# Three small changes around the edges of a tuned kernel: other buffers for the first weights, one product moved up, the last store cut in two

## The chip, the cores and the metric

The kernel runs on one core of one Trainium2 chip. The metric is the device time of that core in microseconds (us), taken over several executions. Every time below was taken beside executions of the kernel before, on the same chip.

In the trace of before, TensorE has 6856 matmul records and as many weight loads, VectorE 998 instructions (696 of them TENSOR_TENSOR), ScalarE 667 (all but one ACTIVATE or COPY) and GpSimd 318 (304 TENSOR_TENSOR). Of the 612 instructions that queue transfers, 562 are SyncE's, 42 ScalarE's and 8 GpSimd's. In the profile PE is TensorE, DVE is VectorE, ACT is ScalarE, POOL is GpSimd, SP is SyncE, and a "q" behind a name means that engine's sequencer.

## The reference

```python
kv  = np.einsum('bhsd,bhse->bhde', k, v)        # batch 8, heads 8, seq 576, head dim 64
out = np.einsum('bhsd,bhde->bhse', q, kv)
rms = np.sqrt(np.mean(out * out, axis=-1, keepdims=True) + 1e-06)
x   = (out / rms * g_norm)                      # -> 4608 x 512
h   = x @ w_in                                  # 512 x 2048, float64 in memory
g   = np.maximum(0.01 * h, h)
y   = g @ w_out                                 # 2048 x 512, float64 in memory
```

## The kernel before

The two weight matrices lie in memory as float64. They are brought in as 32 raw tiles of 512 KB ("load 0" to "load 31"), and each is turned into float32 by a "rounding": ScalarE makes two tensors from the raw words (`add` and `cut`), then VectorE needs four steps for the result. Loads with odd numbers (and 0, but not 31) are tiles of `w_in`, brought by four transfers each; the others are tiles of `w_out`, brought by one. There are seven raw buffers ("homes"), so load j can be issued only after rounding j−7 has read its words:

```python
raw_homes = itertools.cycle([view(stage, i * NW, NW) for i in range(3)]
                            + [pair(i, NW) for i in range(4)])
...
def round_f64(dst, raw):
    ...
    pin(nc.scalar.activation(add, lo, func=AF.Copy, scale=2.0 ** -29))
    pin(nc.scalar.activation(cut, hi.bitcast(F32), func=AF.Copy, scale=2.0 ** -112))
    ...                     # four pinned VectorE steps
```

The four `pair` buffers first hold k and v of the last two pairs of heads of the first batch. Loads 1 and 2 were queued before that batch's kv products (the first part of its attention), loads 3 to 6 after them:

```python
for j in range(1, 3):
    load_w(j)
...                                   # transposes of q
for m in range(2):
    ...
    attention_kv(0, m, kv_ps)
for j in range(3, 7):
    load_w(j)
...
square(1, 1)
spread(0)
add_up(1, 1)
root(1)
```

The first block of tokens then runs in 17 steps. Step n multiplies x by one tile of `w_in` (`h_ps`), applies the leaky relu (a "Prelu" on ScalarE, written `g_n` below), and adds step n−1's product with `w_out` (`o_acc`); the attention of the next batch (batch 1) is spread over the steps. Between the products, `between` issues loads, records roundings, and spreads the attention of the next batch (batch 1) over the steps.

```python
act = nc.scalar.activation(gT, h_ps, func=AF.Prelu, alpha=SLOPE)
if n == 2 * NC * U - 1:
    pin(act)                          # only the last Prelu is pinned
...
while half and rounded < min(3 * n + 8, 2 * n + 13, len(w_jobs) - (n < 11)):
    if loaded < len(w_jobs):
        load_w(loaded)
        loaded += 1
        if loaded in (15, 19):
            load_pair(1, (loaded - 15) // 4)     # q, k, v of batch 1
    round_w(rounded)
    rounded += 1
```

`pin` keeps an instruction in program order among the pinned ones.

Of the kernel before, what the change touches and what calls it, by code (L numbers as in the profile page):

```python
# [23 lines left out]
def kernel(  # L24
# [36 lines left out]
    nc = tc.nc  # L61
    B, H, S, D = q.shape
    DM, DF = w_in.shape
    P = 128
# [6 lines left out]
    NB = B * S // NT  # L71
    N2 = NT // 2
    U = 2
    NC = DF // 2 // (U * P)
# [24 lines left out]
    NW = U * NE * P  # L99
    w1_all = consts.tile([P, 2 * NC * NW], F32, name="w1_all")  # L100
    stage = consts.tile([P, 3 * NW], F32, name="stage")
# [3 lines left out]
    def view(t, lo, *shape):  # L105
        n = 1
        for d in shape:
            n *= d
        t = t[:, lo:lo + n]
        names = "abcd"[:len(shape)]  # L110
        return t.rearrange(f"p ({' '.join(names)}) -> p {' '.join(names)}",
                           **dict(zip(names, shape))) if len(shape) > 1 else t

    def pair(i, *shape):
        return view(pairs, i * NW, *shape)

    def matmul(*args, **kw):
        pin(nc.tensor.matmul(*args, **kw))  # L118
# [86 lines left out]
    def spare(n, name, dtype=F32):  # L205

        return gpool.tile([P, n], dtype, tag=next(spare_homes), name=name)

    raw_homes = itertools.cycle([view(stage, i * NW, NW) for i in range(3)]
                                + [pair(i, NW) for i in range(4)])  # L210

    def load(t, src, eng):

        if len(src.shape) == len(t.shape):
            t, src = [t], [src]
        else:
            n = src.shape[1]
            t = [t[i * n:(i + 1) * n] for i in range(src.shape[0])]
        for i, (to, part) in enumerate(zip(t, src)):
            pin(eng[i * len(eng) // len(t)].dma_start(to, part))  # L220

    def load_f64(src, eng):
        a, n = src.shape[-2:]
        n //= 2
        raw = next(raw_homes).bitcast(U32).rearrange("p (n two) -> p n two", two=2)
        load(raw.rearrange("p (a n) two -> p a (n two)", a=a), src, eng)
        return raw
# [41 lines left out]
    def load_w(j, *eng):  # L269
        eng = eng or (nc.sync,)  # L270
        dst, src = w_jobs[j]
        if w_in.dtype == I64:
            w_raws[j] = load_f64(src.bitcast(U32), eng)
        else:
            load(dst, src, eng)
# [33 lines left out]
    def attention_kv(b, m, kv_ps):  # L309

        two = [(k_ins.pop((b, p)), v_ins.pop((b, p)), p) for p in (2 * m, 2 * m + 1)]
        for j in range(J):
            for i in range(2):
                for k_in, v_in, p in two:
                    r, c = 64 * i, 64 * half_of(p, i)
                    matmul(kv_ps[p % 2][c:c + 64, m, :], lhsT=k_in[r:r + 64, j, :],
                           rhs=v_in[r:r + 64, j, :], start=(j == 0), stop=(j == J - 1))
# [125 lines left out]
    def first_attention():  # L443
# [11 lines left out]


        rest = ps_m.tile([64, NP, P], F32, tag="oc", name="rest_ps")
        for j in range(1, 3):
            load_w(j)

        def move(p, l, to, of):

# [5 lines left out]
        for p in range(NP):  # L468
# [3 lines left out]
            for j in range(J):  # L472
                to = banks[j // 4][:, j % 4, :] if j < 8 else rest[:, p, :]
# [9 lines left out]
        for m in range(2):  # L483
            if m:
                keep_warm()
            attention_kv(0, m, kv_ps)
        for j in range(3, 7):
            load_w(j)
        w0 = rounding(0)
        next(w0, None)  # L490
# [19 lines left out]
        def square(half, l):  # L510
            pin(nc.scalar.activation(squares[half][l], o_ps[half][l], func=AF.Square))
# [9 lines left out]
        def add_up(half, l):  # L521

            for e in range(2):
                matmul(sum_ps[half][E * l:E * l + E, :N2], lhsT=group,
                       rhs=squares[half][l][:, e, :], start=(e == 0), stop=(e == 1))

        def root(half):

            pin(nc.scalar.activation(flat[half], sum_ps[half][:64, :N2], func=AF.Sqrt,
                                     scale=1.0 / D, bias=eps_sb[:64]))  # L530
# [13 lines left out]
        def spread(half):  # L544

            for l in range(2):
                for t in range(2):
                    for p in range(NP):
                        matmul(inv_ps[half][E * p:E * p + E, l, t * P:t * P + P],
                               lhsT=roots[half][:, t, l, p:p + 1].to_broadcast([P, E]),  # L550
                               rhs=ident, start=True, stop=True)
# [17 lines left out]
        for _ in w0:  # L569
            pass  # L570
        square(1, 1)
        spread(0)
        add_up(1, 1)
        root(1)
        turn(1)
        keep(1, 0)
# [11 lines left out]
    def add(eng, out_, a, b_, minus=False, pinned=False):  # L588
        ins = eng.tensor_tensor(out_, a, b_, op=ALU.subtract if minus else ALU.add)  # L589
        if pinned or steady and eng is nc.vector:  # L590
            pin(ins)
# [49 lines left out]
    ORDER = (1, 2, 6, 5, 7, 3, 4)  # L641
# [201 lines left out]
    def product_o(n, g_sides, os, finish):  # L843
        c = n % NC
        w_sides, _ = sides_w2(n)
        sums = sides_w2(n + 1)[1] if n + 1 < NC * (NB - 1) else lambda i: None
        if c == 0:
            for key in ("11", "12", "21", "22"):
                os[key] = opool.tile([P, 2, N2], F32, tag="o", name=f"o{key}", bufs=6)

        into = {1: ("11", True), 5: ("22", True), 2: ("11", False), 6: ("12", True),
                3: ("12", False), 7: ("22", False), 4: ("21", True)}

        def done(i, bank):
            key, fresh = into[i]
            to = os[key].rearrange("p u (v n) -> p (u v) n", v=2)
            if c == 0 and fresh:
                nc.scalar.copy(to, bank)
            else:
                add(nc.vector, to, bank, to)  # L860
            if c == NC - 1 and i in (2, 7, 3, 4):
                finish(key, os[key])

            if i == 5:
                sums(0)
            elif i == 4:
                sums(1)


        yield from strassen((("oa", "oc"), ("oc", "oa"))[n % 2], lambda i, part, r: g_sides[i][:, 2 * r + part, :],  # L870
                            lambda i, part, r: w_sides[i][:, r, :], done)
# [5 lines left out]
            n = None if n is None else n - 1  # L877

    def store(i):
        def finish(key, o):  # L880
            r0 = i * NT + (int(key[0]) - 1) * N2
            c0 = (int(key[1]) - 1) * N2
            nc.scalar.dma_start(
                out[r0:r0 + N2, c0:c0 + N2].rearrange("(t p) m -> p t m", p=P), o)
        return finish

    def first_block(between):
# [28 lines left out]
        for t in range(4):  # L916
# [5 lines left out]
            nc.scalar.dma_start(out[t * P:(t + 1) * P, :], o)  # L922

    first_attention()
    steps = {i: tail for tail in [tail_of(0, NT, S)] for i in (6, 8, 10)}
    a_steps = attention(1, False)
# [50 lines left out]
    for i in range(1, NB):  # L977
# [3 lines left out]
        os = {}  # L981
# [96 lines left out]
```

## Time and profile before

| | before |
|---|---|
| median of three runs | 932.22 us (930.87 to 932.27) |
| span of the profiled run | 929.0 us, mean granted clock 0.999 |
| first feed-forward product (`h_ps`) starts | 26.78 us |
| second kv product of batch 1 (its last two pairs of heads) | 91.55 us, its v landed at 88.92 us |
| last matmul ends | 924.12 us |

A line of the timeline reads: start, duration, engine, source line, operation, output and inputs, shapes, how many, and in brackets how long the engine had stood idle before it and what released it. The prediction shows the lines of the opening. The list of TensorE's waits has the waited-for operation, us in total, number of times, longest.

One line of the list of TensorE's waits: waited-for operation, us in total, number of times, longest.

```profile
PE h_ps L118 <- DVE w_all L255: 0.2, 1, 0.2
```

Before the change a rounded weight is waited for once, for 0.2 us.

### The profile page before, as it was taken

The page shows a single profiled execution, that of the slowest core. Times are in us where ns is not written, and L with a number is a line of the kernel's source. Part 1 is how long each engine was busy: PE and PEld are TensorE (multiplying, and loading weights), DVE is VectorE, ACT ScalarE, POOL GpSimd, SP SyncE. Part 2 cuts the span into 40 slices and gives each one's busy share as a digit, 9 for nine tenths or more (in the row PEclk, how much of TensorE's full clock was granted, in tenths as well). Part 3 has the DMA queues.
Part 4 walks back from the last instruction along what each step waited for, and adds up shares of the span by engine and source line. Part 5 has one row for each costly group of instructions (what it writes and reads, how often), then busy time and mean ns, then how long its engine had stood idle before and what let it go on. Part 6 is the DMA issues. An engine that isn't in the chain of part 4 may idle for free.

```text
span 929.0 us, 17587 instructions
## 1 busy us (share of the span) xinstructions
PE 918.4 (99%) x6856; PEld 776.2 (84%) x6856; DVE 619.2 (67%) x998; ACT 331.0 (36%) x667; POOL 319.0 (34%) x318
## 2 busy tenths in 40 slices
PE   8999999999999999999999999999999999999997
PEld 5544447888998999899989999899988999999996
DVE  4866995586456876597756874687568744654554
ACT  4544632242134332532343423342343333223330
POOL 2000364977522532226211711272225322532222
PEclk9999999999999999999999999999999999999999
DMA  9999926895597679856995599658655676667632
GB/s 258 226 246 239 217 99 199 275 298 165 193 323 245 184 206 300 267 175 190 284 289 180 172 281 293 202 179 256 229 168 177 197 219 185 186 199 221 189 111 91
DMA packets 90066, 200.03 MB, mean 215 GB/s; under 512 B 9856, under 2 KB 42112, under 8 KB 89984
## 3 DMA queue, kind: packets, MB, share of 16 engines
q1 hardware_dynamic: 79392, 186.85, 68.5%
q10 hardware_dynamic: 10144, 10.88, 3.4%
q8 instruction: 55, 0.90, 0.4%
q0 software_dynamic: 448, 1.18, 0.3%
q14 instruction: 27, 0.22, 0.1%
HBM read 172.39 MB, written 26.48 MB: 214 GB/s over the span
## 4 chain that ended last, share of the span: by engine, by line
PE 95%; DMA 2%; DVE 2%; issue 0%; ACT 0%; POOL 0%; ACTq 0%; DVEq 0%; POOLq 0%
PE o_a L118 21%; PE o_c L118 21%; PE h_ha L118 11%; PE h_hb L118 8%; PE h_hc L118 8%; PE h_hd L118 6%; PE o_acc L118 6%; PE h_ps L118 6%; PE o_ps L118 2%; PE kv_ps L118 2%; PE h_a L118 1%; PE h_b L118 1%; DMA pairs<-in_v_dram 1%; PE h_c L118 1%; PE h_d L118 1%; DMA pairs<-in_moe_w_out_dram 1%
## 5 line engine op out<-in xcount | busy, mean ns | idle before, releaser
L589 POOL TENSOR_TENSOR gs<-g 128x512 f32<-128x512 f32 x64 | 81.3, 1289 | 442.9 <-ACT g L760 442.9
L589 DVE TENSOR_TENSOR o<-o_c,o 128x512 f32<-128x512 f32 x104 | 71.6, 689 | 111.8 <-PE o_c L118 111.8
L760 ACT ACTIVATE g<-g 128x512 f32<-128x512 f32 x124 | 78.2, 631 | 120.5 <-DVE g L589 120.5
L824 ACT COPY w_all<-h_ha 128x512 f32<-128x512 f32 x84 | 48.7, 580 | 187.9 <-PE h_ha L118 179.2
L589 DVE TENSOR_TENSOR o<-o_a,o 128x512 f32<-128x512 f32 x88 | 60.5, 687 | 68.0 <-PE o_a L118 67.9
L118 PE MATMUL o_c<-pairs,gs 128*128 128x256 f32 x384 | 91.3, 381 | 0.0
L118 PE MATMUL o_a<-pairs,gs 128*128 128x256 f32 x384 | 90.8, 379 | 0.0
L118 PEld LDWEIGHTS o_c<-pairs,gs 128*128 128x128 f32 x384 | 69.8, 190 | 9.3 <-issue 1.4
L118 PEld LDWEIGHTS o_a<-pairs,gs 128*128 128x128 f32 x384 | 69.8, 190 | 7.8
L118 PE MATMUL o_c<-w,g 128*128 128x256 f32 x256 | 61.6, 383 | 0.0
L118 PE MATMUL o_a<-w,g 128*128 128x256 f32 x256 | 61.6, 383 | 0.0
L118 PEld LDWEIGHTS h_ha<-stage,w_all 128*128 128x128 f32 x448 | 58.7, 192 | 2.8
L118 PE MATMUL h_ha<-stage,w_all 128*128 128x128 f32 x448 | 59.0, 275 | 0.0
L118 PE MATMUL h_ps<-xT,w_all 128*128 128x512 f32 (+1 forms) x136 | 57.9, 570 | 0.2 <-DVE w_all L255 0.2
L118 PE MATMUL o_acc<-w,g 128*128 128x512 f32 x128 | 58.0, 597 | 0.0
L589 DVE TENSOR_TENSOR g<-g,pairs 128x512 f32<-128x512 f32 x84 | 55.6, 689 | 1.9
L118 PEld LDWEIGHTS o_a<-w,g 128*128 128x128 f32 x256 | 46.4, 190 | 11.4 <-ACT pairs L824 2.7
L589 POOL TENSOR_TENSOR pairs<-w_all 128x512 f32<-128x512 f32 x8 | 11.1, 1386 | 123.3 <-DMA stage<-in_moe_w_in_dram 95.4
L118 PEld LDWEIGHTS o_c<-w,g 128*128 128x128 f32 x256 | 46.4, 190 | 5.8
L118 PEld LDWEIGHTS h_ps<-xT,w_all 128*128 128x128 f32 x136 | 25.5, 190 | 29.2 <-issue 26.5
L589 DVE TENSOR_TENSOR g<-w_all 128x512 f32<-128x512 f32 x28 | 21.8, 780 | 40.9 <-ACT w_all L824 40.9
L589 DVE TENSOR_TENSOR w_all<-h_hc,w_all 128x512 f32<-128x512 f32 x56 | 38.4, 686 | 15.3 <-PE h_hc L118 15.0
(193 smaller groups left out, 2039.3 us busy)
## 6 DMA issues: line engine op xcount, KB each, us to landing
w_all<-w SPq DMA_DIRECT2D x196, 448.0 KB, 4.1
pairs<-w SPq DMA_DIRECT2D x56, 512.0 KB, 4.4
out_dram<-o ACTq DMA_DIRECT2D x36, 256.0 KB, 4.6
v_in<-in_v_dram SPq DMA_DIRECT2D x29, 288.0 KB, 5.6
k_in<-in_k_dram SPq DMA_DIRECT2D x28, 288.0 KB, 5.8
q_in<-in_q_dram SPq DMA_DIRECT2D x56, 144.0 KB, 6.4
q_in<-in_q_dram SPq DMA_DIRECT2D x56, 140.0 KB, 6.3
w<-stage SPq DMA_DIRECT2D x12, 512.0 KB, 4.6
```

The source lines that it names most:

```text
L118: pin(nc.tensor.matmul(*args, **kw))
L589: ins = eng.tensor_tensor(out_, a, b_, op=ALU.subtract if minus else ALU.add)
L760: nc.scalar.activation(t, t if src is None else src, func=AF.Prelu, alpha=SLOPE)
L824: nc.scalar.copy(q[:, at], banks[tag])
```

## The change

It has three parts. First, the homes are rotated so that loads 1 to 4 land where k and v stood, and loads 1 to 6 are all queued after the kv products of the first batch: the early weights should stay out of the way of the opening. Second, the last sums of squares go ahead of the first spreading on TensorE. Third, the last store is cut in two halves on two queues.

```diff
-    raw_homes = itertools.cycle([view(stage, i * NW, NW) for i in range(3)]
-                                + [pair(i, NW) for i in range(4)])
+    raw_homes = itertools.cycle([view(stage, 0, NW)] + [pair(i, NW) for i in range(4)]
+                                + [view(stage, i * NW, NW) for i in (1, 2)])
...
-        for j in range(1, 3):
-            load_w(j)
...
-        for j in range(3, 7):
+        for j in range(1, 7):
             load_w(j)
...
         square(1, 1)
+        add_up(1, 1)
         spread(0)
-        add_up(1, 1)
...
+                for part in range(2) if last else ():
+                    two = slice(2 * part, 2 * part + 2)
+                    add(nc.vector, to[:, two, :], bank[:, two, :], to[:, two, :])
+                    finish(key, os[key], part)
...
+            if part is not None:
+                r0 += part * P
+                (nc.sync, nc.scalar)[part].dma_start(out[r0:r0 + P, c0:c0 + N2], o[:, part, :])
+                return
```

More of the change, by code (lines that the diff above doesn't have):

```diff
@@ L859, in done @@
             else:
+                last = n + 1 == NC * (NB - 1) and i == ORDER[-1]
+                for part in range(2) if last else ():
+                    two = slice(2 * part, 2 * part + 2)
+                    add(nc.vector, to[:, two, :], bank[:, two, :], to[:, two, :])
+                    finish(key, os[key], part)
+                if last:
+                    return
                 add(nc.vector, to, bank, to)
@@ L879, in store, with finish @@
     def store(i):
-        def finish(key, o):
+        def finish(key, o, part=None):
             r0 = i * NT + (int(key[0]) - 1) * N2
             c0 = (int(key[1]) - 1) * N2
+            if part is not None:
+                r0 += part * P
+                (nc.sync, nc.scalar)[part].dma_start(out[r0:r0 + P, c0:c0 + N2], o[:, part, :])
+                return
             nc.scalar.dma_start(
```

## The prediction

> **What bounds the kernel now.** I read the page first: busy shares, then the chain that ended last.
>
> ```profile
> PE 918.4 (99%) x6856; PEld 776.2 (84%) x6856; DVE 619.2 (67%) x998; ACT 331.0 (36%) x667; POOL 319.0 (34%) x318
> ...
> PE 95%; DMA 2%; DVE 2%; issue 0%; ACT 0%; POOL 0%; ACTq 0%; DVEq 0%; POOLq 0%
> ```
>
> TensorE carries 95% of the chain, and the granted clock is 9 tenths or more in every slice. In the list of waits over the whole span TensorE has only nine entries, and eight lie before 31 us. So the end is: the moment TensorE starts the first feed-forward product, plus a fixed stretch of matmuls (26.78 to 924.13 us in the timeline), plus the tail. A change in the opening counts only as far as it moves the 26.78; the third part counts only after 924.13. The change adds and removes no matmul, so the middle stays. I therefore read the timeline of the opening:
>
> ```profile
> 13.64 1.40 PE L118 MATMUL kv_ps<-pairs 64*64 64x64 f32 x72 [0.27 <-DMA pairs<-in_v_dram]
> ...
> 15.51 1.17 PE L118 MATMUL o_ps<-qT,kv 64*32 64x256 f32 x27 [0.47 <-DVE kv L321]
> ...
> 17.81 1.49 PE L118 MATMUL o_ps<-qT,kv 64*32 64x256 f32 x37 [1.13 <-issue]
> ...
> 18.48 1.57 ACT L511 ACTIVATE sq<-o_ps 128x512 f32<-128x512 f32 x3 [1.18 <-PE o_ps L118]
> ...
> 21.08 0.58 ACT L511 ACTIVATE sq<-o_ps 128x512 f32<-128x512 f32 x1
> ...
> 22.25 1.08 PE L118 MATMUL inv_ps<-ident,roots 128*32 128x128 f32 x32 [0.42 <-DVE roots L542]
> ...
> 23.16 1.03 PE L118 MATMUL sum_ps<-sq,group 128*32 128x256 f32 x4
> ...
> 24.22 0.47 ACT L529 ACTIVATE flat<-sum_ps,eps_sb 64x256 f32<-64x256 f32 x1 [2.57 <-PE sum_ps L118]
> ...
> 25.46 0.26 DVE L542 RECIPROCAL roots<-sum_ps 128x16 f32<-128x16 f32 x1 [1.37 <-ACT xT L519]
> ...
> 25.77 1.08 PE L118 MATMUL inv_ps<-ident,roots 128*32 128x128 f32 x32 [0.42 <-DVE roots L542]
> ...
> 26.78 3.72 PE L118 MATMUL h_ps<-xT,w_all 128*128 128x256 f32 x16
> ```
>
> Two things are to be seen. First, the last squares are ready at 21.08 + 0.58 = 21.66, but their sums (four records at 23.16) stand behind the first spreading at 22.25; ScalarE idles 2.57 us for them, and the second half (root, turn, reciprocal, second spreading, h_ps) hangs on that. Second, the o_ps products stop between their 27th and 28th record. Each product leaves two records, so the stop is inside one product[...]. It has no releaser ("issue"). The trace's transfers show the queue of kind "instruction" bringing its first 16,384 bytes at 14.94 us, taking 1.27 us. I read the stop as TensorE out of instructions. The chain view skips from 18.12 to 24.57 through a weight transfer; ScalarE at 24.59 simply follows its root at 24.22, so I don't use that step.
>
> The tail: the last VectorE add runs from 924.16 to 924.85 and the last store is issued at 924.88. Of its 16 landing counts, 15 come between 926.85 and 927.09 and the last at 927.82. In that stretch the instruction queue brings its last 16,384 bytes (925.25, 1.03 us). One DMA engine is late, the one with instructions.
>
> [...]1.27 us at 14.94, amid weights, against 0.88 to 0.96 us for the fetches at 175, 192, 237 and 267 us. [...]at 124.97, while GpSimd adds, one rounding step took 1.75 us instead of 0.69.
>
> **Part 1, the homes.** Before, loads 1 and 2 had stage buffers of their own and were queued early: the pieces of load 1 issued at 10.13 to 13.68 and it landed at 18.86. After, load 1 goes where k of pair 2 stood, so it waits for the last kv matmul (about 15.05) and all six loads follow. Did load 1 delay k and v? I counted transfer starts by size: the last k and v packets start near 12.2 and land by 13.51; up to 14 us the 1024-byte packets are at most 0.39 MB, less than load 0 alone (0.52 MB). So load 1 stood behind k and v and took nothing from them: 0 us there. But between 14 and 17 us DMA moved 351, 220 and 203 GB/s, most of it loads 1 and 2, just when the instruction fetch ran. After the change it has almost only the end of load 0 beside it. I take 1.27 to about 0.9 us (0.37)[...]: the stop of 1.5 us between starts (16.30 to 17.80) shrinks by 0.8, an estimate from those durations. It lies on the path: squares wait 1.18 us for o_ps. ScalarE is busy rounding load 0 until 17.30, so at most 1.2 can be used.
>
> The price: the weights start later. With about 0.9 us from issue to first byte, 2.3 us for each 512 KB (loads 3 to 7 landed 1.9 to 2.9 apart) and 1.2 of receipt, load 1 lands near 19.6, 2 at 21.8, 3 at 24.2, 4 at 26.4, about 1 us later than now. Rounding reads now start at 26.02, 27.15, 28.29, 29.43, with 7.2, 6.3, 4.6 and 3.9 us in hand. Reads come 1.8 earlier, landings 1 later: load 4 keeps about 1 us. Cost 0.
>
> **Part 2, the order.** With the rest unmoved: squares end 21.65, plus 0.15 (as from 19.07 to 19.22) gives the sums at 21.80; four records 0.216 apart, the last taking 0.38, end 22.83. Root 22.87 to 23.34. The first spreading moves from 22.25 to 22.68 and ends at 23.76 instead of 23.33. The turn follows at 23.59 and ends at 24.20. VectorE scales at 23.83 (instead of 23.40), overlapping slightly with the reciprocal at 24.43 (now 25.46), because the reciprocal is behind that scaling. The second spreading starts at 24.75 instead of 25.77: 1.0 us gained, where the sums alone would have given 1.35. The second rounding follows the last scaling on VectorE, so it moves too and h_ps number two (30.67) gains the same.
>
> **Part 3, the store.** Two adds of 256 columns start about 0.34 apart (as the 128x256 adds at 149.09 and 149.43) and end at 924.53 and 924.92; SyncE issues at 924.56, ScalarE at 924.96. I don't expect the first add to start before the bank is complete: the scaling at 23.40 needed half of inv_ps and waited for all of it. Without the late engine the second half, 128 KB at 0.34 MB/us, would end 0.4 us earlier. But both halves give the late engine the same 16 KB beside the same instruction block. I count 0.1.
>
> Sum: 0.8 + 1.0 + 0.1 = 1.9 us. From the median 932.22 of before (three runs, 930.87 to 932.27): 930.3; the lower run and the profiled one (930.69) pull a little, so 930.2.
>
> **Rivals.** (a) *The fetch is not eased*: its 3 us run-up may be fixed; then only the order pays, about 1.1 us, 931.1. For it: a fetch at 81.7 also took 1.33. Against: that, too, was beside weights. (b) *The weights become the bound*: if the stream starts 2 us later than I think, load 4 is late, ScalarE holds the first Prelu behind it, and the gain is gone, 932 or a little more. Against: o_acc reads that Prelu only at 34.18, 3 us later. (c) *The rotated homes move GpSimd's work*: pair 0, where sides of the first Strassen weights go, comes free after load 29 instead of 31, pair 2 after 31 instead of 26. GpSimd's adds from 101.75 to 138.45 shift among VectorE's, each clash costing about 1 us of VectorE. For it: 1.75 against 0.69. Against: GpSimd idles 13 us afterwards and TensorE never waits there; 0, at worst 1 us lost. (d) *The tail gains fully*, if the last fetch falls elsewhere: 0.5 more, 929.8.
>
> **Range and chances.** Best case 1.2 + 1.1 + 0.6 gives 929.3, with run scatter 928.4; worst, (b) or (c) with scatter, 932.2. Two per cent is 18.6 us, more than the whole opening can give back, and nothing above costs so much: within 2% at 0.98.
>
> **What would show it.** The sums before the spreading and the second spreading about 1.0 us earlier relative to the end of the last square; the o_ps stop near 0.7 us instead of 1.5; h_ps from about 25.0; loads 1 to 4 landing before they are read; TensorE unbroken until about 922.3; one of the last landings still 0.5 us or more behind. It would be wrong if k and v land earlier, if the stop stays, or if ScalarE waits for a weight transfer.

## More of the kernel before

What isn't pinned is put into the engine's queue where the program's own static scheduler places it when the program is built. Roundings and transfers are pinned, the Prelus of the first block are not.

## The result, and the profile after

| | runs | median, us | lowest to highest |
|---|---|---|---|
| before | 6 | 931.05 | 929.50 to 932.27 |
| after | 6 | 936.10 | 931.84 to 936.89 |

The ratio of after to before is 1.0049, 95% interval 1.0027 to 1.0070. A ratio here is the mean time of one kernel's runs over the mean of the other's from the same rounds, so it isn't quite the ratio of the medians. Within 2% was right, but the change made the kernel about 5 us slower, where the prediction had it 2 us faster and its range ended at 932.2.

The profiled run of after took 935.88 us, with a span of 934.2 us and a mean clock of 0.997. First its page: TensorE's busy time, share and number of records, next to the chain of work that ended last.

```profile
PE 921.1 (99%) x6856; PEld 777.2 (83%) x6856; DVE 620.4 (66%) x999; ACT 331.1 (35%) x667; POOL 318.4 (34%) x318
...
PE 88%; DMA 2%; DVE 1%; ACT 0%; issue 0%; DVEq 0%; SPq 0%
```

The same 6856 records are busy 2.7 us longer, and the span is 5.2 us longer. So TensorE both waited somewhere and ran slower somewhere. The opening, in the timeline:

```profile
15.17 2.50 PE L118 MATMUL o_ps<-qT,kv 64*32 64x256 f32 x64 [0.52 <-DVE kv L322]
...
20.82 0.38 PE L118 MATMUL sum_ps<-sq,group 128*32 128x256 f32 x1
...
23.05 1.08 PE L118 MATMUL inv_ps<-ident,roots 128*32 128x128 f32 x32 [0.44 <-DVE roots L541]
24.06 1.13 PE L118 MATMUL h_ps<-xT,w_all 128*128 128x256 f32 x4
```

The opening did better than predicted. The 64 o_ps records run in one piece (before they were 27 and 37 with an idle time of 1.13 us between), the last sums of squares are done before the spreading, and `h_ps` starts at 24.06 instead of 26.78 us: 2.72 us gained. So the loss lies later. The list of TensorE's waits over the whole span:

```profile
PE kv_ps L118 <- DMA v_in<-in_v_dram: 2.4, 1, 2.4
PE h_ps L118 <- DVE w_all L256: 2.3, 4, 0.9
```

Both are new: four waits for rounded weights instead of one, and one for v. I compared the start of every group of TensorE in the two traces; "offset" is after minus before.

| point in the kernel | before, us | after, us | offset |
|---|---|---|---|
| `h_ps` of step 0 | 26.78 | 24.06 | −2.72 |
| step 3 | 44.48 | 41.76 | −2.72 |
| step 4 | 51.81 | 49.75 | −2.06 |
| step 5 | 59.15 | 58.27 | −0.88 |
| step 6 | 66.02 | 66.15 | +0.13 |
| second kv product of batch 1 begins | 91.55 | 91.78 | +0.24 |
| first `h_ps` after that kv product | 96.29 | 100.86 | +4.57 |
| after the first stores, near 151 us | 151.30 | 156.46 | +5.16 |
| last matmul ends | 924.12 | 929.25 | +5.13 |

Steps 4 to 6 cost 3.0 us, the second kv product 4.3, a spot near 150 us 0.6, the tail 0.1. Together that is 7.9 from −2.7, which is the 5.2 of the spans.

Why do steps 4 to 6 wait? Here is ScalarE's timeline around 40 us, first before, then after. `add` opens a rounding, `g` is a Prelu.

```profile
36.00 0.68 ACT L242 ACTIVATE add<-pairs 128x512 uint32<-128x512 uint32 x1
...
37.13 0.69 ACT L242 ACTIVATE add<-stage 128x512 uint32<-128x512 uint32 x1
...
41.24 0.60 ACT L905 ACTIVATE g<-h_ps 128x512 f32<-128x512 f32 x1 [2.85 <-PE h_ps L118]
41.74 0.67 ACT L242 ACTIVATE add<-stage 128x512 uint32<-128x512 uint32 x1
```

```profile
33.28 0.66 ACT L243 ACTIVATE add<-stage 128x512 uint32<-128x512 uint32 x1
...
38.53 0.60 ACT L916 ACTIVATE g<-h_ps 128x512 f32<-128x512 f32 x1 [4.03 <-PE h_ps L118]
39.02 0.66 ACT L243 ACTIVATE add<-stage 128x512 uint32<-128x512 uint32 x1
...
45.39 0.60 ACT L916 ACTIVATE g<-h_ps 128x512 f32<-128x512 f32 x1 [5.15 <-PE h_ps L118]
...
46.09 0.68 ACT L243 ACTIVATE add<-stage 128x512 uint32<-128x512 uint32 x1
```

Before, roundings 6 and 7 (36.00 and 37.13) stand ahead of the Prelu at 41.24. After, rounding 6 starts at 39.02, behind that Prelu, and rounding 7 at 46.09, behind the next one, though ScalarE stood idle for 4.03 and 5.15 us just before those Prelus. The raw words weren't late: load 6 had landed at 32.72 and load 7 at 35.33 us. Load 7 is the weight tile of step 4. Its rounding ends on VectorE at 49.69 us, and step 4 starts at 49.75.

So the two kernels have another order in ScalarE's queue. I read it from the built programs (r is a rounding, g a Prelu; from g7 on they are alike):

```
before: r0 r1 r2 r3 r4 g0 g1 r5 r6 r7 g2 r8 g3 r9 r10 g4 r11 r12 g5 r13 r14 g6 r15 ...
after:  r0 r1 r2 g0 r3 g1 r4 r5 g2 r6 g3 r7 r8 g4 r9 r10 g5 r11 r12 g6 r13 r14 r15 ...
```

Nothing in the diff asks for that. Programs built with one part each show that the homes alone bring the order of after, and that the other two parts don't. ScalarE kept to the built order in the trace: it idled for 5.15 us until 45.39 with the words of rounding 7 there since 35.33, ran the Prelu that stood ahead of that rounding, and only then, at 46.09, the rounding.

The late roundings also free their homes later, so the loads behind them are issued later (load 15 at 50.61 instead of 48.26, load 18 at 63.75 instead of 57.83), and k and v of batch 1 stand behind those in the same queue. In the timeline, TensorE's second kv product before and after:

```profile
91.55 1.28 PE L118 MATMUL kv_ps<-v_in,k_in 64*64 64x64 f32 x72
```

```profile
91.78 0.33 PE L118 MATMUL kv_ps<-v_in,k_in 64*64 64x64 f32 x2
94.51 1.75 PE L118 MATMUL kv_ps<-v_in,k_in 64*64 64x64 f32 x70 [2.40 <-DMA v_in<-in_v_dram]
```

Before, v had landed at 88.92. After, it landed at 94.38. The wait is 2.40 us, but the offset grows by 4.3. The windows view of after gives the rest. Its columns are: the stretch, its length, TensorE's busy time with the number of records, the granted clock, the DMA share, GB/s.

```profile
94.50:97.50 3.00, 2.99 (x72) 0.60 0.74 208
97.50:101.00 3.50, 3.50 (x8) 0.86 1.10 240
```

After the wait TensorE's clock was granted at 0.60 and then 0.86, and it was 1.00 on both sides of that. These two stretches cut across the steps of the clock. Cut at the steps, which lie a multiple of 3.41 us apart in the trace (clock records of 88.75 us at 1.00, 3.41 at 0.50 and 832.85 at 1.00), the same view reads:

```profile
91.68:95.09 3.41, 1.01 (x40) 1.00 0.92 184
95.09:98.51 3.42, 3.42 (x50) 0.50 0.89 254
```

The whole wait lay in the first of them, and in the next the clock was half. So 1.9 us came on top of a wait of 2.4 us. By estimate 1.7 of it is the clock: half of the 3.42 us that were granted 0.50.

### The profile page after: what moved, and what is told of

Read it like the earlier page. It is cut to its first block, busy times and chain, and to the rows that moved or that the text cites. A ratio compares the mean times of both kernels' runs of the same rounds, so it can differ in the third digit from the quotient of the medians.

```text
span 934.2 us, 17589 instructions
## 1 busy us (share of the span) xinstructions
PE 921.1 (99%) x6856; PEld 777.2 (83%) x6856; DVE 620.4 (66%) x999; ACT 331.1 (35%) x667; POOL 318.4 (34%) x318
## 3 DMA queue, kind: packets, MB, share of 16 engines
q0 software_dynamic: 448, 1.18, 0.3%
## 4 chain that ended last, share of the span: by engine, by line
PE 88%; DMA 2%; DVE 1%; ACT 0%; issue 0%; DVEq 0%; SPq 0%
PE o_a L118 21%; PE o_c L118 21%; PE h_ha L118 11%; PE h_hb L118 8%; PE h_hc L118 8%; PE h_hd L118 6%; PE o_acc L118 3%; PE h_ps L118 2%; PE o_ps L118 2%; PE kv_ps L118 2%; PE h_a L118 1%; PE h_b L118 1%; PE h_c L118 1%; PE h_d L118 1%; DMA v_in<-in_v_dram 1%; DMA pairs<-in_moe_w_out_dram 1%
## 5 line engine op out<-in xcount | busy, mean ns | idle before, releaser
L588 DVE TENSOR_TENSOR o<-o_c,o 128x512 f32<-128x512 f32 (+1 forms) x105 | 71.7, 683 | 111.5 <-PE o_c L118 111.4
L118 PEld LDWEIGHTS o_acc<-w,g 128*128 128x128 f32 x128 | 24.3, 194 | 29.8 <-issue 29.3
```

What stands on the lines that cost most here:

```text
L118: pin(nc.tensor.matmul(*args, **kw))
L588: ins = eng.tensor_tensor(out_, a, b_, op=ALU.subtract if minus else ALU.add)
```

## The experiments

Each kernel was timed in five rounds beside the kernel before and profiled. Four were run at a time on one chip. The medians of before in the four sittings were 931.61 (11 runs, 928.91 to 937.38: the widest), 930.92, 930.87 and 930.65 us.

| run | what it is | median, us | lowest to highest | ratio to before, 95% interval |
|---|---|---|---|---|
| homes_alone | part 1 | 938.50 | 934.62 to 940.44 | 1.0062 (1.0033 to 1.0091) |
| order_alone | part 2 | 930.53 | 927.67 to 932.96 | 0.9986 (0.9960 to 1.0013) |
| tail_alone | part 3 | 930.76 | 929.78 to 931.39 | 0.9993 (0.9981 to 1.0005) |
| order_tail | parts 2 and 3 | 929.77 | 928.79 to 931.01 | 0.9989 (0.9976 to 1.0002) |
| late_rounding | before, roundings behind the Prelus nearly as in after | 936.03 | 932.10 to 940.22 | 1.0047 (1.0018 to 1.0077) |
| put_back | after, Prelus in the order of before | 930.64 | 928.78 to 937.23 | 0.9998 (0.9966 to 1.0030) |
| put_back_2 | the same again | 931.33 | 928.05 to 936.82 | 1.0008 (0.9981 to 1.0035) |
| before_kv_first | before, two loads behind k, v, q | 937.67 | 937.60 to 939.38 | 1.0075 (1.0062 to 1.0088) |
| after_kv_first | after, the same | 940.13 | 938.15 to 942.58 | 1.0095 (1.0079 to 1.0111) |
| put_back_kv_first | put_back, the same | 937.04 | 936.58 to 938.03 | 1.0061 (1.0048 to 1.0074) |
| kv_first_put_back | that, Prelus held further | 937.50 | 936.39 to 938.38 | 1.0071 (1.0058 to 1.0084) |
| before_kv_put_back | before_kv_first, Prelus held | 939.91 | 937.53 to 940.65 | 1.0090 (1.0074 to 1.0106) |
| kv_gpsimd_put_back | put_back, k and v on GpSimd's queue | 938.85 | 936.99 to 942.37 | 1.0087 (1.0070 to 1.0104) |
| before_kv_held | before_kv_first, whole order held | 931.46 | 930.04 to 932.51 | 1.0003 (0.9989 to 1.0018) |
| homes_held | part 1, whole order held | 932.87 | 930.38 to 937.65 | 1.0031 (1.0005 to 1.0057) |
| kv_first_held | after, two loads behind, whole order held | **928.13** | 926.72 to 929.01 | 0.9967 (0.9953 to 0.9982) |

### First question: which part, and is it the order?

The theory for the first four runs was the order of ScalarE's queue. The rival was the loads: they start later, and somebody waits for them.

**homes_alone** keeps only the first three hunks of the diff (homes and loads).

> Only the first part of the change: the homes. Theory A (the static order of ScalarE's queue is what costs): the instruction order built for this kernel already puts roundings 3 and 4 behind the first two Prelus and every later one up to 13 a Prelu later, as in the whole change, so the stalls must all be here: TensorE reaches the first h_ps about 1.6 us earlier than before (25.2 instead of 26.78), but steps 4, 5 and 6 of the first block wait for the rounded weights (about 3 us together) and the second kv product of the next batch waits for v (about 4 us); the time is 5 to 7 us above before. Rival B (the loads simply start later and DMA is the limit): the same sign, but then a weight's rounding would start right when its load lands; A expects it 1 to 20 us after the landing. Rival C (GpSimd's shifted sums): no wait before 100 us, and all of the loss after it.

It measured 938.50 us. In its trace `h_ps` starts 1.46 us earlier than before, steps 4 to 6 wait as in after, and the second kv product waits 4.5 us for v. Part 1 alone carries the loss, and more of it than the whole change.

**order_alone** has only this:

```diff
+        add_up(1, 1)
         spread(0)
-        add_up(1, 1)
```

> Only the second part: the last sums of squares ahead of the first spreading. ScalarE's static order is as before. All theories: first h_ps about 1.1 us earlier than 26.78, the o_ps products still stop about 1.5 us after their 27th record, no new wait later; time 0.7 to 1.2 us under before. If the reorder by itself set off the loss, the time would be above before.

It measured 930.53, with an interval of the ratio that includes 1. In its own profile the opening was even later than before's, because the o_ps stop was longer there:

```profile
18.11 2.78 PE L118 MATMUL o_ps<-qT,kv 64*32 64x256 f32 x37 [2.31 <-issue]
```

The stop's length changes from run to run (see below), so the order is judged from the end of the o_ps records to `h_ps`: 7.48 us in before, 6.57 here, 6.39 in after. (After that long stop the clock was 0.50 from 18.14 to 21.55 us here, so 6.57 is rather too long.)

**late_rounding** puts the roundings behind the Prelus in the kernel before, as after has them. The edges carry no semaphore; they only tell the scheduler what goes first:

```diff
+    AHEAD = {0: 3, 1: 4, 2: 6, 3: 7, 4: 9, 5: 11, 6: 13}
+    def ahead(act, n):                        # rounding AHEAD[n] behind Prelu n
+        if n in AHEAD:
+            tc.add_manual_dep(adds[AHEAD[n]].ins, act.ins.name, NoSync, ...)
...
+                ahead(act, n)
```

> The kernel before with nothing of the change but ScalarE's static order of the change (roundings 3, 4, 6, 7, 9 and 11 tied behind Prelus 0 to 5); homes, loads and stores as before. Theory A: the waits of steps 4 to 6 appear (about 3 us), loads from the 15th on are issued later and v of the next batch is late again (about 4 us); without the opening's gain the time is 5 to 8 us above before, about 937. Rivals B and C: no change, within 1 us of before.

It measured 936.03 us: 4.7 thousandths slower than before, where after was 4.9. Homes, order of the products and store are those of before. The queue isn't quite that of after: the last edge had no effect (rounding 13 still runs ahead of g6), and VectorE's order, which nothing held, moved along. The orders of TensorE, SyncE and GpSimd are those of before. The list of TensorE's waits has both entries of after:

```profile
PE kv_ps L118 <- DMA v_in<-in_v_dram: 2.4, 1, 2.4
...
PE h_ps L118 <- DVE w_all L265: 1.3, 3, 0.7
```

So the late roundings, with VectorE's order moving along and nothing else changed, cost 4.4 us between the medians. This is not yet the whole loss of after, which lost 7.9 us after its opening; its 5 us are what a gain of 2.7 us left of them. In late_rounding's profile, 4.8 us were lost after the opening: 2.1 in steps 4 to 6 and 2.7 at v, which lands at 96.95 us there.

**put_back** is the reverse: the whole change, with the first seven Prelus put behind the roundings that they stood behind before.

```diff
+    BEHIND = {0: 4, 1: 4, 2: 7, 3: 8, 4: 10, 5: 12, 6: 14}
+    def behind(act, n):                       # Prelu n behind rounding BEHIND[n]
+        if n in BEHIND:
+            tc.add_manual_dep(act.ins, cuts[BEHIND[n]].ins.name, NoSync, ...)
```

> The whole change, but with ScalarE's static order put back to that of before (each of the first seven Prelus tied behind the rounding that it followed before; nothing else changes: the orders of TensorE, SyncE and GpSimd are those of the change). Theory A: the opening keeps its 2.7 us, the waits of steps 4 to 6 and the wait for v are gone, at most the 0.6 us near 150 us stays; time 2 to 2.7 us under before, about 928.6. Rival B (late loads): ScalarE now waits in its queue for loads 3 to 7, the Prelus behind them are late, and the time stays 3 us or more above before. Rival C: the loss stays too.

The median is 930.64 us: the 5 us are gone. Steps 4 to 6 no longer wait; the entry in TensorE's list is that of before again:

```profile
PE h_ps L118 <- DVE w_all L265: 0.2, 1, 0.2
```

The 2.14 us that this run gained in its opening last until 88 us. But the kernel is no faster than before, its runs spread over 8.5 us, and in the profile (of its slowest run, 937.23) the second kv product waits longer than in after:

```profile
96.42 2.19 PE L118 MATMUL kv_ps<-v_in,k_in 64*64 64x64 f32 x70 [5.82 <-DMA v_in<-in_v_dram]
```

The rival is right here, in part. ScalarE now reaches loads 3, 4, 6 and 7 within 0.11 us of their landing, and v lands at 96.28 us. (VectorE's order isn't that of before here either; only ScalarE's was tied.)

**put_back_2** repeated that kernel for another profile.

> The same kernel as put_back, for another profile and five more rounds. Theory: its spread is the wait for v, so in a profile of a run near 929 v of the fourth pair lands before about 90 us and TensorE has no entry for v_in above 0.5 us; in a run above 933 it has one of 3 us or more. Rival: a fast and a slow run have the same waits on TensorE and differ elsewhere.

The six runs spread again (928.05 to 936.82), and again the profiled one was the slowest: a wait of 5.3 us for v, which landed at 95.26. A fast run of this very kernel was never profiled. That its fast runs find v in time is therefore not shown for it, but a near relative (homes_held, below) shows it.

Why v is late in these runs can be followed along SyncE's queue. Of 70 transfers in a row, from load 5 to that v, 64 in put_back and 60 in put_back_2 were issued within 0.35 us of the landing of the eighth transfer before them. In before it was 45 and in after 38 of 70; there the stream is held back by the roundings. In none of the 18 traces does this queue have more than eight transfers under way. So here the stream has no spare time left: those 64 and 60 transfers followed the last of the 16 landing counts of an earlier one by at most 0.35 us. For the transfers issued between 20 and 50 us the median time between the first and the last count was 2.6 us in before, 3.1 in homes_held, 3.7 in put_back and 5.1 in put_back_2. What makes the last count lag more in one run than in another stayed open.

### Second question: take the wait for v away

If the wait for v is what remains, k, v and q should be queued earlier. Loads 23 and 24 can wait behind them:

```diff
-            if loaded < len(w_jobs):
-                load_w(loaded)
+            while loaded < min(rounded + 3, 23 if n == 5 else len(w_jobs)):
+                load_w(loaded)
```

**after_kv_first**, **put_back_kv_first** and **before_kv_first** have this on the three kernels.

> The whole change, and the loads of rounding jobs 23 and 24 queued behind k, v and q of the second two pairs of batch 1 instead of ahead of them. Theory: of the 7.9 us that the changed kernel lost between 24 us and its end (from 2.7 us early at the first feed-forward product to 5.1 us late), 3.0 are the waits of steps 4 to 6 for roundings, 4.3 the wait of the second kv product for v, 0.6 a wait near 150 us. Then here only the 4.3 go: v lands before 92 us instead of at 94.4, TensorE has no entry for v_in in its waits, and the median is 931 to 932.5. Rival: v is only where a stream that is short of bandwidth shows first; then the two loads that now come last are waited for instead (an entry of TensorE for w_all after 95 us) and the median stays at 935 to 936.

> The whole change, ScalarE's order of before forced as in put_back, and the loads of jobs 23 and 24 behind k, v and q. Theory: put_back had runs from 928.8 to 937.2 because its stream of loads has no spare time left and v lands before or after 92 us from run to run; with v ahead the 2.1 us of the opening are kept in every run: median 928 to 929.5, no run over 932. Rival: the spread has another cause (a run-to-run lag of the DMA engine that also fetches instructions, which delays whatever is loaded last): the spread stays at 8 us and the median at about 930.6.

> The kernel before with only the two loads behind k, v and q. Theory: in a usual run of before v lands 2.6 us ahead of its use (88.9 against 91.6), so the median moves by less than 0.7 us; if the one run of before at 937.4 was the wait for v, no run is above 933. Rival: SyncE now stands at k until the first kv product has read its tile (74.3 us) with the two loads behind it, so weights 25 and on come 2 us later and something waits for them: 1 to 2 us slower.

All three expectations failed in the total: 940.13, 937.04 and 937.67 us. Yet the wait for v was gone in all three traces. The offset of put_back_kv_first was still −2.36 at 128 us; by 148 us it was +7.50. Even the kernel before lost 6.7 us by queuing two loads later. New waits for rounded weights had appeared near the end of the first block, up to 4.9 us in one piece in put_back_kv_first and 5.8 in before_kv_first. The raw words again were not late: in before_kv_first the loads 25 to 31 were read 14.7 to 25.7 us after landing. The built program again had another order (r23 and r24 now behind g10, r25 and r26 behind g11, r27 and r28 behind g12, r29 to r31 behind g13).

That was the same trap. The next two runs held the order, but only that of the Prelus against the roundings: **kv_first_put_back** on the whole change, **before_kv_put_back** on before. The edges are those of put_back, continued:

```diff
-    BEHIND = {0: 4, 1: 4, 2: 7, 3: 8, 4: 10, 5: 12, 6: 14}
+    BEHIND = {0: 4, 1: 4, 2: 7, 3: 8, 4: 10, 5: 12, 6: 14, 10: 24, 11: 26, 12: 28, 13: 31}
```

> As put_back_kv_first, but ScalarE's order of before is forced up to the end of the first block (the Prelus of steps 10 to 13 behind roundings 24, 26, 28 and 31, too). Theory: put_back_kv_first lost its 9.9 us only because the moved loads made the static order push the roundings 23 to 31 behind later Prelus (its loads had landed 9 to 18 us before they were read). With the order held, neither v nor w_all is waited for: the 2.4 us of the opening last to the end, median 928 to 929, no run above 931. Rival: the two loads that now come last (landed at 91.8 there) are read too early in that order and hold ScalarE, or VectorE's order, which moves too, makes TensorE wait: 930 or more, with an entry of TensorE for w_all, g or kv after 90 us.

> Before with loads 23 and 24 behind k, v and q as in before_kv_first, ScalarE's order of before held to the end of the first block. Theory: the 6.7 us of before_kv_first were the order alone; here 930.9 as before, within 0.7 us. Rival: they came of the later transfers themselves (SyncE standing at k until 74.3 us) or of VectorE's order: 934 or more.

Both missed again, 937.50 and 939.91 us. The trace of kv_first_put_back shows why, in ScalarE's timeline and in TensorE's:

```profile
105.45 0.98 ACT L359 ACTIVATE sum<-o_ps 128x448 f32<-128x448 f32 x2 [7.26 <-PE o_ps L118]
106.32 1.16 ACT L365 ACTIVATE xT<-o_ps,g_sb 128x448 f32<-128x448 f32 x2
107.35 0.69 ACT L252 ACTIVATE add<-pairs 128x512 uint32<-128x512 uint32 x1
```

```profile
134.63 5.40 PE L118 MATMUL h_ps<-xT,w_all 128*128 128x512 f32 x8 [2.81 <-DVE w_all L265]
...
143.20 3.75 PE L118 MATMUL o_acc<-w,g 128*128 128x512 f32 x4 [3.17 <-DVE w L265]
```

ScalarE stands for 7.26 us at squares of batch 1's attention (`sum`), and rounding 25 (107.35) is behind them. Before, rounding 25 started at 100.42, ahead of them. Load 25 had landed at 97.01. With k and v queued earlier, the scheduler had moved the attention's own instructions forward, and I had held only the Prelus. The delayed roundings bunched up on VectorE beside GpSimd's sums: from 128 to 142 us single steps of a rounding took 0.9 to 1.6 us, where at 118 us they took 0.4 to 0.7.

**kv_gpsimd_put_back** took k and v of the last two pairs to GpSimd's queue, with the Prelus held in the same way:

```diff
+            way = nc.gpsimd if b == 1 and p > 1 else nc.sync
-            k_ins[b, p] = load_two(nc.sync, k[b, 2 * p:2 * p + 2], in_tile("k"))
+            k_ins[b, p] = load_two(way, k[b, 2 * p:2 * p + 2], in_tile("k"))
```

> The whole change, ScalarE's order of before forced to the end of the first block, and k and v of the second two pairs of batch 1 on GpSimd's queue, so that they stand behind no weight in SyncE's queue and don't wait for one of its eight transfers to land. Theory: v lands before 88 us and the wait of the second kv product goes; median 928 to 929, no run above 931. Rival: the engines are as full on another queue and v still lands after 92 us, or a weight instead is late: spread and median of put_back (930.6, up to 937).

It measured 938.85 us. The second kv product of batch 1 didn't wait, so that half of the theory held. Load 25 was read at 107.89, 12.6 us after it had landed, and TensorE lost 9.9 us at the end of the block (offset −1.79 at 129 us, +8.12 at 149).

### Third question: hold the whole order

The last kernels hold all of ScalarE's and VectorE's instructions of the first block in the order of before. Each instruction is noted as it is recorded, and consecutive ones of the wanted order are tied without a semaphore:

```diff
+    def hold_order():
+        for eng, runs in ROWS.items():                 # the order read from the built program of before
+            row = [done_by[eng][i] for a, b in runs for i in range(a, b) if i < len(done_by[eng])]
+            for a, b in zip(row, row[1:]):
+                tc.add_manual_dep(b.ins, a.ins.name, NoSync, ...)
```

**before_kv_held** is before with the two loads moved and this.

> Before with loads 23 and 24 behind k, v and q and the whole order of before held on ScalarE and VectorE. Theory: only the order cost 6.7 to 9 us in before_kv_first and before_kv_put_back: here 930.9 as before, within 0.7 us. Rival: the transfers cost it: 934 or more.

It measured 931.46 us, ratio 1.0003. The same moved loads with a free order had cost 6.7 us. So the transfers themselves cost nothing measurable there; the order had cost everything.

**homes_held** is part 1 alone with the order held.

> Part 1 alone with the whole order of before held. Theory: the first feed-forward product starts 1 to 1.5 us earlier than before's, the waits of steps 4 to 6 for w_all are gone, but the loads run 2 to 3 us later than before's, so v is late in some runs: median 929.5 to 932, with runs above 934. Rival: the homes cost nothing once the order is held: median 929.5 to 930 and no run above 932.

It measured 932.87 us, in two groups: three runs at 930.4 to 930.6, three at 935.2 to 937.7. The profiled run was a fast one (930.38). In it v landed at 88.93 us and was used at 90.32:

```profile
90.32 1.28 PE L147 MATMUL kv_ps<-v_in,k_in 64*64 64x64 f32 x72
```

That is 1.4 us to spare, against 2.6 in before. But even this run ends only 0.24 us ahead of before (last matmul 923.88), of the 1.23 that it gained in its opening. It lost the other 0.99 at one matmul that before passes without a stop:

```profile
147.44 1.97 PE L147 MATMUL h_a<-xt,pairs 128*128 128x256 f32 x8 [0.75 <-issue]
```

So with the order held, part 1 gains in the opening, loses most of that again near 147 us, and depends besides on whether v comes in time.

**kv_first_held** is the whole change, the two loads behind k, v and q, and the order held.

> The whole change, loads 23 and 24 behind k, v and q, and the whole order of before held on ScalarE and VectorE through the first block, not the Prelus alone. Theory: then no queue holds a rounding behind something that comes later; no wait for v, none for w or w_all: h_ps 2 to 2.4 us early and so to the end: median 928 to 929, no run above 931. Rival: the loads themselves come too late when they stand behind k, v and q (23 and 24 landed at 92.1 and 94.5, the instant ScalarE reached them) or GpSimd's sums, whose order isn't held, collide with VectorE: 931 or more, with TensorE waiting for w or w_all after 120 us.

It measured 928.13 us with no run above 929.01, and 0.9967 (0.9953 to 0.9982) of before: 2.5 us between the medians, and faster than both kernels. Its list of TensorE's waits has nothing of v, and the kv product runs nearly in one piece (L102 is the line of the helper that notes the instructions):

```profile
PE o_ps L147 <- issue: 0.4, 1, 0.4
PE h_ps L147 <- DVE w_all L102: 0.2, 1, 0.2
```

```profile
89.36 1.53 PE L147 MATMUL kv_ps<-v_in,k_in 64*64 64x64 f32 x72
```

`h_ps` starts 2.19 us earlier than in before; 0.25 is lost at that kv product (v landed at 89.48) and 0.38 in a later kv product near 171 us. The stop near 147 us of homes_held isn't there.

### The store

**tail_alone** has only part 3, **order_tail** parts 2 and 3.

> Only the last store in two halves on two queues. Theory: each half still gives a share to the DMA engine that brings the last block of instructions, so the last landing stays about 1 us behind the other fifteen and the time moves by less than 0.3 us either way. Rival: the halves gain the 0.4 us by which the first is issued earlier, or 0.7 with the engine free: 0.4 to 0.7 us faster, and the last counts of both halves within 0.3 us of the others.

> Parts 2 and 3 without the homes. Theory: the two add, 1.0 us of order and 0.1 to 0.4 of the store (0.4 where the last block of instructions comes at another time): 1.1 to 1.4 us faster than before, no wait for v or w_all. Rival: moved 1 us ahead, TensorE reaches v of the next batch or a weight earlier than it lands in some runs: runs at 933 and above, median within 0.5 us of before.

tail_alone measured 930.76 (0.16 less than before beside it), order_tail 929.77 (1.1 less); the interval of order_tail ends at 1.0002, so its gain is likely but not quite certain. The profiles tell more than these medians, since the tail can be measured from the last matmul's end. The table sorts them by when the last block of instructions (16,384 bytes) was fetched, in us after the last matmul:

| store | profile | fetch begins | last landing |
|---|---|---|---|
| whole | before | +1.14 | +3.70 |
| whole | homes_held | +1.18 | +3.63 |
| whole | order_alone | +5.10 | +2.97 |
| whole | late_rounding | +5.15 | +2.97 |
| halves | after | +1.24 | +3.80 |
| halves | kv_first_held | +1.10 | +3.65 |
| halves | tail_alone | +4.99 | +2.61 |
| halves | order_tail | +4.74 | +2.63 |
| halves | put_back | −1.66 | +2.92 |

The halves of after, in its timeline, with the two adds ahead of them:

```profile
929.29 0.76 DVE L588 TENSOR_TENSOR o<-o_c,o 128x256 f32<-128x256 f32 x2 [1.03 <-PE o_c L118]
929.75 0.34 SPq L892 DMA_DIRECT2D out_dram<-o  x1
930.08 0.35 ACTq L892 DMA_DIRECT2D out_dram<-o  x1
```

Where the fetch doesn't meet the store, the halves gain 0.36 us (2.97 to 2.61). Where it does, one landing count of each half comes about 1.2 us behind the others (15 of 16 landed by 931.84, the last at 933.06), and the halves gain nothing. The trace's packets show the late ones. In after the fetch ends at 931.53; from 931.51 to 932.25 eight packets of 1,024 bytes of the first half run one behind the other, then eight of the second half until 932.59, while all others had ended by 931.48. In before the fetch ends at 926.29, and the last 13 of the whole store's 256 packets run in such a row from 926.71 to 927.34. The 16 late packets of after are a sixteenth of its 256, and one of the 16 landing counts of each half is late. The nine profiles that aren't in the table agree. In put_back_kv_first the fetch begins at +1.13 and the halves land at +3.60. With the fetch elsewhere the whole store lands at +2.97 or +2.98 (four profiles) and the halves at +2.59 to +2.62 (three). In after_kv_first, with the fetch at −0.91, the halves land at +2.86, much as in put_back; why those two lie in between stays open. When the fetch comes is not set by the change: it fell into both places with both kinds of store.

## Why the prediction was wrong

**The step that failed is "Cost 0", the price of part 1, together with "so the middle stays".** The prediction compared the landings of loads 1 to 4 with the moments at which before had read them, and stopped there. Two things were missing. It took the order of ScalarE's queue as given, although the Prelus are not pinned and the order is made anew for each build. Late roundings cost 4.4 us between the medians without any of the change (late_rounding). And it didn't follow the stream of transfers to its end at 94 us, where v of the next batch had 2.6 us to spare. In place of 0, the profiled run lost 7.9 us after the opening: 3.0 in steps 4 to 6, 4.3 at v (2.4 of waiting and 1.9 after it, with 3.42 us at a clock of 0.50), 0.6 near 150 us and 0.1 in the tail. The waits of steps 4 to 6 are shown to be the reordering in both directions: late_rounding brings them, put_back takes them away. The wait for v has two causes that can replace each other: late roundings, which brought 2.7 us at v to the kernel before, and, with the order put back, a stream without spare time (64 and 60 of 70 transfers issued within 0.35 us of a landing), whose landings lag by a different amount in each run (a median of 3.7 us in put_back, 5.1 in put_back_2). Held order and an earlier v together take both waits away (kv_first_held). VectorE's order moved with ScalarE's in late_rounding and put_back, so the two were not told apart. Why the scheduler chose this order (I think it expects the raw words later, when their transfers stand later in the queue) is argued from the builds, not shown.

**Rival (b), "the weights become the bound", had the right engine and the wrong sense.** It expected ScalarE to hold a Prelu behind a late load. What happened was a rounding behind an early-placed Prelu, with its load landed 6 to 17 us before. The rival's own case came true only once the order was put back: loads 3 and 4 were then read 0.11 and 0.08 us after landing, and TensorE didn't notice. The prediction had left load 4 about 1 us in hand. In after the loads 1 to 4 landed at 20.14, 22.85, 25.52 and 27.75 us, 0.5 to 1.4 later than its sum said. The 0.9 and the 1.2 us in that sum are near the trace of before: from issue to first packet 1.07 us for load 2 and 0.90 for the last store, and from the start of the last packet to the last landing count 1.13 to 1.16 us for loads 2, 4 and 6.

**Rival (c), GpSimd's moved work, may be the 0.6 us near 150 us, which the prediction had as "0, at worst 1 us lost".** They come with the homes. The same matmul (`h_a<-xt,pairs`) loses 0.5 to 1.0 us in all five profiles with the new homes, loads 23 and 24 in their old place and no other trouble late in the block: after 0.59, homes_alone 0.97, homes_held 0.99, put_back 0.54, put_back_2 1.03. It doesn't in any of the eight with the old homes. In after, a transfer of ScalarE's waited for the landing of an earlier one at 151.70, and GpSimd's sums had ended near 142 us, their transfers running from 140 to 150. But kv_first_held has the new homes too and no such loss, so the cause stays open.

**Part 1's gain, "0.8", was mis-sized.** Of the 0.8, 0.37 came from the durations of fetches; the rest was my estimate, with no trace behind it. It measured 1.28 us for the stop in this pair of profiles, and about 1.3 on average. Another 0.34 came from k and v that landed earlier (13.06 instead of 13.51 us), but that is scatter: over all 18 profiles they land at 12.73 us on average with the old homes and at 12.71 with the new ones. So the prediction's "0 us there" stands. That the stop is the fetch is well supported, though nothing changed the fetch alone. In the eight profiles with the old homes the first fetch took 1.17 to 1.28 us and began at 14.88 or later, and the idle time inside the o_ps products was 0.9 to 2.6 us, 1.8 on average. In the ten with the rotated homes it took 0.88 to 0.94 us, began by 14.66, and the idle time was 0 to 1.3, 0.5 on average. The prediction's own comparison, with quiet fetches at 175, 192, 237 and 267 us, doesn't hold: beside those at 175, 192 and 267 us DMA moved 331, 246 and 285 GB/s, more than the 215 at 14.94. Beside the first fetch itself it moved 193 to 252 GB/s with the old homes and 0 to 131 with the new. TensorE resumed 1.3 to 1.8 us after the end of that packet in the traces of before, order_alone, late_rounding, homes_alone and put_back.

**Part 2's "1.0 us gained" was right:** from the last o_ps record to `h_ps` 7.48 us before, 6.39 after, so 1.09. In order_alone and order_tail, with a clock of 0.50 for a while after a longer stop, it was 6.57 and 6.77.

**Part 3's "0.1" was right in its reason, the late landing (1.2 us behind in each half of after), but nothing was gained:** in after's profile the tail grew by 0.1. The gain is 0.36 in runs where the fetch comes at another time, as rival (d) said, which had 0.5 more than the 0.1.

**Of the signs it named,** the loads 1 to 4 did land before they were read, and the sums came ahead as drawn. "TensorE unbroken until about 922.3" failed first at step 4, and that is where the reading of the result began.

## What to carry to other kernels

When a scheduler places part of an engine's queue, moving a transfer or a buffer can reorder work that the diff doesn't mention. Compare the order of each queue in the two built programs before judging a change, and pin or tie the order that was tuned. A gain ahead of a stream that runs without spare time is only kept if the last transfer of that stream still lands in time (put_back lost its 2.14 us at a wait of 5.82 us for v), so follow the stream to its end. And count a stop of TensorE at more than its length if the clock falls with it: in after 2.40 us of standing still within one stretch of 3.41 us were followed by 3.42 us at 0.50, and the offset grew by 4.3 us.

## What the traces show of the fetch, the clock and the order

- The queue of kind "instruction" brought 55 packets of 16,384 bytes in before (0.90 MB). If the stop of the o_ps products is the first of these fetches (the profile names no releaser), it cost TensorE time: TensorE stood 0.9 to 2.6 us in eight profiles with weight transfers beside the fetch, and 0 to 1.3 in ten with fewer. With a fetch beside it the last store landed 0.7 us later (3.70 in before against 2.97 us after the last matmul in order_alone). In put_back, a SyncE instruction that queues a transfer took 2.48 us at 18.09, while a block that took 2.48 us was being fetched from 17.95.
- A wait of 2.40 us was followed by a mean granted clock of 0.60 over 3.0 us and 0.86 over the next 3.5 (after), and one of 2.38 us in late_rounding left the 70 records at full pace (1.27 us). A wait of 5.35 us in put_back_2 was followed by 0.50 over 2.6 us. All 18 traces show more. Cut them into stretches of 3.41 us, counted from the start of each clock record. Then of the stretches at full clock, the 15 in which TensorE stood for 2.08 us or more were each followed by one at 0.50, and the 4,805 in which it stood for 1.87 us or less were followed by one at 1.00. The wait of after lay wholly in one stretch, that of late_rounding in two (0.60 and 1.78 us). The stretch of after was not idle as a whole: TensorE was busy for 1.01 of its 3.41 us. On top of the wait for v the runs paid 0.3 to 3.2 us (late_rounding 0.3, after 1.9, homes_alone and put_back 3.2).
- Queue order made at build time moved here when only buffers and transfers moved. Roundings put behind Prelus cost 4.4 us between the medians in late_rounding, and a held order was worth 6.2 us between the medians of before_kv_first and before_kv_held.
